# Attention with memory slots and a routed feed-forward: two sets of four batches become batches that start eight chunks apart, in an order computed by a time model

## The chip, the cores and the metric

One Trainium2 chip, one core. The metric is device time in microseconds (us) of one execution. TensorE (PE) multiplies, its weight loads are PEld, VectorE is DVE, ScalarE is ACT, GpSimd is POOL, SyncE is SP; SP and POOL also issue the DMAs, each from a queue in program order.

## The reference

B = 8 batches, H = 8 heads, S = 576 rows, head width 64, M = 32 memory slots, D = 512, F = 1024, capacity 128. All data are float32.

```python
a = exp(phi - max(phi, axis=2));  a = a / (sum(a, axis=2) + 1e-9)     # over the 576 rows
k_m = einsum('bhsm,bhsd->bhmd', a, k);  v_m = einsum('bhsm,bhsd->bhmd', a, v)
attn = softmax(q @ k_m.T / 8)                                          # over the 32 slots
x = (attn @ v_m) as (B, S, 512)
scores = x @ w_gate
for b in range(B):                                                     # the 128 rows of highest score
    xe = x[b, top]
    out[b, top] = xe + sigmoid(scores[b, top]) * (relu(xe @ w1) @ w2)  # the other rows: out = x
```

## The kernel before

Per batch there is a chain of stages. `softmax` computes `a` with 20 DVE instructions over 128x1152 (the two halves g of the heads, 576 rows each) and shorter ones, with ACT instructions between them that it waits for. `split_v` cuts each v piece (four per batch) into a high part and a rest on DVE (L285, L287) and stores each part twice in the DRAM buffer `vparts` (L290, four issues a piece on POOL's queue). `keys` turns `a` with 12 transposes (L303), splits it (L309, L311), stores each part twice in `aparts` (L314), and multiplies with k (L322) to the keys kT.

`values(st)` makes v_m for a set `st` of four batches at once. One matmul takes one row s of one batch: 32 partitions (4 head pairs, high and low part of both factors) by 128 columns, and the four batches sit in four groups of 32 partitions, so four matmuls follow each other into four row groups of the array (L371). A chunk is T = 24 rows of four batches, 96 matmuls; a set has 24 chunks. Chunks go through NB = 2 pairs of buffers: two DMAs from POOL (L345) fill `v_rows`, eight from SP (L350) fill the diagonal blocks of `a_rows`, whose other entries are zero. The first set can start when four batches are keyed, the second when eight are.

`attention(b)` needs v_m of b: `centre`, `scores`, `attend` (L505, L522 on PE, L526 to L497 on DVE), `rank` (L548, L566), `gather` (L585, and the chosen rows by an indirect DMA, L594). `ffn` multiplies 128 gathered rows with w1 and w2 (L610, L622, L629) and scatters the result (L636). In `attention`, `mean` waits until all 8 batches are keyed.

The order of instructions on every engine is the order in which these generators are advanced: two of the 16 jobs (8 softmax chains, then 8 attentions) are live at a time, and after each step of one, `split`, `sums` (the values), `weights` and `feed` (the feed-forward) get steps at fixed rates:

```python
jobs = [batch(b) for b in range(B)] + [attention_beside(b) for b in range(B)]
...
steps("sums", rows_summed, 1.5 if late else 4)
if late:
    steps("weights", weights, 1)
    steps("feed", feed, 0.6)
```

The functions in full:

Of the kernel before, what the change touches and what calls it, by code (L numbers as in the profile page):

```python
# [24 lines left out]

# [15 lines left out]
Y0_BIAS = 14 * 0.6931471805599453  # L41


@with_exitstack
def kernel(
# [14 lines left out]
    nc = tc.nc  # L60
# [13 lines left out]
    T = 24  # L74
    NB = 2
# [11 lines left out]
    accp = ctx.enter_context(tc.tile_pool(name="accp", bufs=1, space=PSUM))  # L87
    pss = ctx.enter_context(tc.tile_pool(name="pss", bufs=4, space=PSUM))
    ex = ctx.enter_context(tc.tile_pool(name="ex", bufs=2))
    work = ctx.enter_context(tc.tile_pool(name="work", bufs=2))  # L90
    one = ctx.enter_context(tc.tile_pool(name="one", bufs=1))

    def bank(shape, dtype=F32):
        return pss.tile(list(shape), dtype, tag="bank", name="bank")
# [3 lines left out]
    def load_phi(b):  # L98
        phis[b] = ex.tile([P, NG, S], F32, name="ph", bufs=3)
        for g in range(NG):  # L100
            nc.sync.dma_start(out=phis[b][:, g], in_=phiT[b, g])

    def load_k(b, g):
        ks[b, g] = ex.tile([PT, NPR, NC, Dh], F32, name="kb")
        nc.sync.dma_start(out=ks[b, g].rearrange("p h c d -> p h (c d)"), in_=k[b, g])

    def load_q(b, j):
        qs[b, j] = ex.tile([P, NPR, S // 2], F32, name="qb", tag="ph", bufs=3)
        nc.sync.dma_start(out=qs[b, j], in_=qT[b, :, :, j * (S // 2):(j + 1) * (S // 2)])
# [4 lines left out]
    make_identity(nc, ident)  # L114

    kT = [const.tile([P, NPR, M], F32, name=f"kT{i}") for i in range(B)]
    vbd = [const.tile([P, NG, NPR, Dh], F32, name=f"vbd{i}") for i in range(3)]


    v_rows = [rows.tile([P, T, NG, Dh], F32R, name=f"v_rows{i}") for i in range(NB)]  # L120
    a_rows = [rows.tile([P, NPR, T, M], F32R, name=f"a_rows{i}") for i in range(NB)]
    for t in v_rows + a_rows:
        nc.gpsimd.memset(t.bitcast(F32), 0.0)
    for t in vbd:
        nc.gpsimd.memset(t, 0.0)

    wg = const.tile([P, D], F32, name="wg")
    ident16 = const.tile([P, P], BF16, name="ident16")
# [5 lines left out]

    tgs = [const.tile([P, NT, 2], F32, name=f"tg{i}") for i in range(3)]

    def late_consts():
        nc.sync.dma_start(out=wg, in_=bass.AP(
            tensor=w_gate.tensor, offset=w_gate.offset,
            ap=[[0, P]] + [list(x) for x in w_gate.ap]))  # L140
# [17 lines left out]

    def constant(value):
        t = const.tile([P, 1], F32, name=f"c{len(biases)}")  # L160
        nc.gpsimd.memset(t, value)
        return t


    biases = {}
    for x in (EXP_P[2], EXP_P[1], EXP_Q[1], SQ_B, 1.0, 127 * 2.0 ** 23, Y0_BIAS):
        biases[x] = constant(x)
# [4 lines left out]
    tt, stt = nc.vector.tensor_tensor, nc.vector.scalar_tensor_tensor  # L172
    soft = {}

    def softmax(b):

        def t(name, dtype=F32):
            return ex.tile([P, NG * S], dtype, name=name)

        ph = phis.pop(b)  # L180
        r = ph.rearrange("p g s -> p (g s)")
        mx = ex.tile([P, NG], F32, name="mx")
        nc.vector.tensor_reduce(mx, ph, axis=AX.X, op=ALU.max)  # L183
        for g in range(NG):
            nc.vector.tensor_scalar(out=ph[:, g], in0=ph[:, g], scalar1=mx[:, g:g + 1],
                                    scalar2=EXP_LOWEST, op0=ALU.subtract, op1=ALU.max)
# [3 lines left out]
        for ln2 in (LN2_HI, LN2_LO):  # L190
            stt(out=r, in0=q, scalar=-ln2, in1=r, op0=ALU.mult, op1=ALU.add)
        act(rh, r, 1 / GRID)
        num = t("num")
        act(num, r, SQ_S, SQ_B, AF.Square)
# [601 lines left out]
```

## Time and profile before

| | before |
|---|---|
| runs of the kernel | 911.61 us median of 3 (907.06 to 912.07) |
| profiled execution, its own time | 907.15 us |
| span in its trace | 905.3 us |
| PE / DVE / ACT / POOL busy | 547.1 / 548.2 / 222.6 / 258.7 us |
| DMA | 165.55 MB, mean 183 GB/s |

The span is what the trace covers; the execution's own time has 1.85 us more. Busy shares are averages over stages with different limits; the stages are told apart in the slices and windows below.

### The profile page before, as it was taken

How to read it: one execution, taken by the hardware profiler on the slowest of the kernel's cores; microseconds unless marked ns; L12 is line 12 of the kernel's file. 1: busy time of each engine (PE TensorE's matmuls, PEld its weight loads, DVE VectorE, ACT ScalarE, POOL GpSimd, SP SyncE). 2: the span in 40 equal slices, each digit the busy share in tenths (PEclk: the TensorE clock that was granted, in tenths of full speed). 3: DMA queues.
4: the chain of work that ended last, by engine and by line, in shares of the span. 5: the costliest groups of instructions: out<-in, count | busy, mean ns of one | idle time of the engine just before them, and what ended most of it. 6: DMA issues, size and time to landing. Idle time of an engine off the chain costs nothing.

```text
span 905.3 us, 16762 instructions
## 1 busy us (share of the span) xinstructions
PE 547.1 (60%) x6917; PEld 449.3 (50%) x6918; DVE 548.2 (61%) x803; ACT 222.6 (25%) x369; POOL 258.7 (29%) x373
## 2 busy tenths in 40 slices
PE   0010020202066568774859999987999798598595
PEld 0010020202065568774728787865885675476373
DVE  8997999999965386655914336206225347748800
ACT  2423242525213124222310120300210223134210
POOL 7245353425335224224142213223223011101100
PEclk9999999999999555557585555868569799589888
DMA  3569899896998677857777755546255433111200
GB/s 103 169 246 321 267 310 293 268 306 228 292 266 259 173 226 233 225 172 210 239 214 224 233 171 167 159 125 209 69 165 175 123 94 99 64 38 64 76 21 18
DMA packets 61409, 165.55 MB, mean 183 GB/s; under 512 B 12816, under 2 KB 21008, under 8 KB 61328
## 3 DMA queue, kind: packets, MB, share of 16 engines
q0 software_dynamic: 30080, 108.02, 37.2%
q1 hardware_dynamic: 31248, 56.39, 21.3%
q8 instruction: 57, 0.93, 0.4%
q14 instruction: 24, 0.20, 0.1%
HBM read 96.21 MB, written 68.16 MB: 182 GB/s over the span
## 4 chain that ended last, share of the span: by engine, by line
PE 45%; DVE 27%; DMA 15%; SPq 5%; issue 4%; POOL 1%; ACT 1%; DVEq 0%; POOLq 0%; ACTq 0%
PE acc L371 19%; PE bank L622 8%; DMA a_rows<-aparts 7%; PE bank L629 5%; SPq L350 5%; PE bank L522 4%; DMA aparts<-aS 3%; PE bank L505 3%; DVE mx L183 2%; DMA vparts<-vlo 2%; DVE vlo L287 2%; PE bank L585 2%; DVE ph L252 2%; DMA aparts<-alo 1%; PE bank L303 1%
## 5 line engine op out<-in xcount | busy, mean ns | idle before, releaser
L371 PE MATMUL acc<-a_rows,v_rows 32*128 32x128 f32 x4608 | 234.5, 374 | 114.1 <-DMA a_rows<-aparts 87.8
L371 PEld LDWEIGHTS acc<-a_rows,v_rows 32*128 32x128 f32 x4608 | 220.0, 285 | 142.6 <-issue 125.3
L345 POOL DMA_DIRECT2D v_rows<-vparts x96 | 92.4, 967 | 287.6 <-PE acc L371 278.6
L303 PE MATMUL bank<-ident,ph 128*96 128x128 f32 x96 | 23.3, 421 | 148.5 <-DVE ph L254 148.5
L303 PEld LDWEIGHTS bank<-ident,ph 128*96 128x96 f32 x96 | 17.5, 197 | 152.2 <-issue 145.6
L622 PE MATMUL bank<-xeT,w 128*128 128x128 f32 x512 | 78.4, 309 | 2.6 <-ACT xeT L612 2.1
L622 PEld LDWEIGHTS bank<-xeT,w 128*128 128x128 f32 x512 | 70.5, 216 | 8.3 <-ACT xeT L612 3.2
L290 POOL DMA_DIRECT2D vparts<-vlo x64 | 35.6, 559 | 123.6 <-DVE vlo L287 112.6
L566 DVE SCALAR_TENSOR_TENSOR marks<-row,tg,wide 128x576 bf16<-128x576 f32 x40 | 32.7, 818 | 58.6 <-ACT row L552 57.2
L526 DVE TENSOR_TENSOR xj<-bank,rd 128x512 f32<-128x512 f32 x40 | 27.3, 688 | 62.6 <-PE bank L522 62.4
L629 PE MATMUL bank<-w,hT 128*128 128x512 f32 x128 | 65.1, 647 | 0.0
L522 PE MATMUL bank<-vbd,eT 128*128 128x256 f32 x160 | 58.6, 505 | 0.3 <-ACT vbd L430 0.3
L206 DVE TENSOR_TENSOR num<-num,lin 128x1152 f32<-128x1152 f32 x16 | 21.7, 1358 | 37.8 <-ACT lin L170 36.5
L522 PEld LDWEIGHTS bank<-vbd,eT 128*128 128x128 f32 x160 | 36.7, 248 | 11.9 <-issue 5.0
L290 POOL DMA_DIRECT2D vparts<-vb x64 | 35.9, 565 | 9.6 <-DMA aparts<-aS 9.3
L629 PEld LDWEIGHTS bank<-w,hT 128*128 128x128 f32 x128 | 25.0, 206 | 24.2 <-issue 23.0
L533 POOL DMA_DIRECT2D out<-xj x24 | 16.2, 673 | 60.7 <-DVE xj L529 44.9
L634 DVE SCALAR_TENSOR_TENSOR ye<-bank,gr,xe 128x512 f32<-128x512 f32 x8 | 6.0, 748 | 43.7 <-PE bank L629 43.7
L430 ACT ACTIVATE vbd<-bank 32x128 f32<-32x128 f32 x32 | 8.6, 268 | 96.2 <-PE bank L426 95.9
L510 DVE TENSOR_SCALAR rd<-bank 128x40 f32<-128x40 f32 x8 | 1.6, 199 | 50.5 <-PE bank L505 50.5
L564 ACT ACTIVATE marks<-row,tg 128x576 bf16<-128x576 f32 x40 | 30.9, 773 | 1.3
L322 PE MATMUL bank<-kb,aS 96*32 96x64 f32 x768 | 19.3, 285 | 17.7 <-ACT aS L304 17.7
(128 smaller groups left out, 938.3 us busy)
## 6 DMA issues: line engine op xcount, KB each, us to landing
v_rows<-vparts POOLq DMA_DIRECT2D x96, 384.0 KB, 5.8
vparts<-vlo POOLq DMA_DIRECT2D x64, 288.0 KB, 4.3
vparts<-vb POOLq DMA_DIRECT2D x64, 288.0 KB, 5.2
a_rows<-aparts SPq DMA_DIRECT2D x384, 48.0 KB
vb<-in_v SPq DMA_DIRECT2D x32, 288.0 KB
kb<-in_k SPq DMA_DIRECT2D x16, 576.0 KB
aparts<-alo POOLq DMA_DIRECT2D x32, 288.0 KB, 7.9
aparts<-aS POOLq DMA_DIRECT2D x32, 288.0 KB, 8.5
```

The lines of the kernel that those rows point to most:

```text
L290: nc.gpsimd.dma_start(out=view(vparts[g, b, t, w], c), in_=src)
L303: nc.tensor.transpose(out=tp[:, c], in_=a[:, c0 + c], identity=ident)
L345: nc.gpsimd.dma_start(out=vr[g::2, :, g], in_=vparts[g, b0:b0 + SET].rearrange("b t w j s d -> (b t w j) s d")[:, ss])
L350: nc.sync.dma_start(out=ar[2 * j + g::8, j].rearrange("p s m -> p (s m)"), in_=aparts[g, j, b0:b0 + SET].rearrange("b t w s m -> (b t w) ( ...
L371: nc.tensor.matmul(out=accs[bb][:, :P].rearrange("p (j m) -> p j m", m=M), lhsT=vr[p, s].rearrange("p g d -> p (g d)"), rhs=ar[p, :, s], s ...
L505: nc.tensor.matmul(out=den[:, c, g], lhsT=eT[:, g, c * P:(c + 1) * P], rhs=heads_of, start=True, stop=True)
L522: nc.tensor.matmul(out=o[:, g * 4 * Dh:(g + 1) * 4 * Dh], lhsT=eT[:, g, (c0 + c) * P:(c0 + c + 1) * P], rhs=vbd[b % 3][:, g].rearrange("p ...
L526: nc.vector.tensor_mul(x[:, c].rearrange("p (h d) -> p h d", d=Dh), o.rearrange("p (h d) -> p h d", d=Dh), rd[:, c0 + c].unsqueeze(2).to_b ...
L564: nc.scalar.activation(sign, row, AF.Sign, bias=g, scale=-1.0, accum_out=less[:, c:c + 1])
L566: nc.vector.scalar_tensor_tensor(out=cmp, in0=row, scalar=g, in1=wide[:, off:off + S], op0=ALU.is_equal, op1=ALU.mult, accum_out=equal[:, ...
L622: nc.tensor.matmul(out=ps[:, f, :n], lhsT=w1_sb[d][:, (f0 + f) * P:(f0 + f + 1) * P], rhs=xeT[:, d, :n], start=(d == 0), stop=(d == KD - 1))
L629: nc.tensor.matmul(out=ps[:n], lhsT=hT[:, f, :n], rhs=w2_sb[f // 2][:, f % 2], start=(f == 0), stop=(f == KF - 1))
```

## The change

1. **Lagged batches.** `values` is one walk over 88 chunks of T = 18 rows. Batch b enters at chunk 8b and leaves 32 chunks later, so chunks 0 to 7 hold one batch, 8 to 15 two, 24 to 63 four, and 80 to 87 one again. The result of batch b is there at chunk 8b + 31. The roles of the two operands are swapped (a is the stationary one), so v_m takes one more transpose per batch.
2. **Compact rows, widened on chip.** Four DMAs from SP bring the chunk's compact `a_flat` (NF = 3 buffers); one POOL instruction and three ACT instructions of 128x576 multiply it with a 0/1 column (`block_of`) into the four blocks of `a_rows`.
3. **v stored once.** `vparts` and `aparts` hold each part once; the loads read it twice by a stride of zero. 64 instead of 128 stores of v, 32 instead of 64 of a.
4. **Order from a time model.** Every engine call goes through `Noted`, which adds a modelled duration to that engine's modelled time (`Plan`); `in_order_of_time` always advances the generator whose next step is ready first. Two softmax chains (batches 0, 2, 4, 6, 7 and 1, 3, 5) and two attentions are live side by side. `split_v` starts a piece at the earliest every 11 modelled us.
5. **Feed-forward.** `forward` starts when all v pieces are split, all weights have come and batch 7's `a` is turned (its buffer becomes hT), and is advanced when nothing else has PE's next free time.
6. Smaller: PSUM banks are taken and given back by hand, `mean` no longer waits for all batches, the score of a pair of row tiles is made one tile at a time, in `keys` the matmuls go through one head after the other, and the cast to `ident16` and the 28 warming matmuls are gone.

```diff
+    def array(self, cycles, used, mode):
+        start = max(self.free.get("pe", 0.0), self.t if self.last in (None, "pe") else self.end)
+        per = self.speed(start)
...
+def in_order_of_time(plan, jobs):
+    live = [[0.0, bias, job, None] for bias, job in jobs]
...
+        x = min(able, key=lambda x: max(x[0], plan.free.get("pe", 0.0)) if x[1] is None else x[0] - x[1])
...
-    T = 24
-    NB = 2
+    T = 18
+    NB, NV, NF = 2, 2, 3
+    LAG = S // T // SET
+    COLS = ((B - 1) * LAG + S // T) * T
...
-        nc.vector.tensor_copy(ident16, ident)
...
             for w, src in enumerate((lo, vb)):
-                for t in range(2):
-                    nc.gpsimd.dma_start(out=view(vparts[g, b, t, w], c), in_=src)
+                nc.gpsimd.dma_start(out=view(vparts[g, b % SET, :, w, c0:c0 + S], c), in_=src)
...
+    def a_loader():
...
+                    nc.sync.dma_start(
+                        out=a_flat[ch % NF][32 * r0 + 2 * t + g:32 * r1:4]
+                            .rearrange("p s m -> p (s m)"),
+                        in_=src[:, ch * T * M:(ch + 1) * T * M].unsqueeze(1)
+                            .to_broadcast([(r1 - r0) * NPR, 2, T * M]))
...
+    def v_loader():
...
+            while ch - NV >= len(used_up) or len(flat) < ch:
+                yield lambda: ch - NV < len(used_up) and len(flat) >= ch
...
+                nc.gpsimd.dma_start(
+                    out=v_rows[ch % NV].bitcast(F32)[32 * r0 + g:32 * r1:2, g]
...
+    def widener():
...
+                if j < 1:
+                    nc.gpsimd.tensor_scalar_mul(ar[:, :, j], src, block_of[:, j:j + 1])
+                else:
+                    nc.scalar.activation(ar[:, :, j], src, AF.Copy, scale=block_of[:, j:j + 1])
...
+    def values():
+        for ch in range(COLS // T):
...
+            for s in range(T):
+                for b in live(ch):
+                    p = slice(b % SET * 32, b % SET * 32 + 32)
+                    nc.tensor.matmul(out=accs[b % SET][:, :P].rearrange("p (g d) -> p g d", d=Dh),
+                                     lhsT=ar[p, s].rearrange("p j m -> p (j m)"), rhs=vr[p, :, s],
...
-        while len(keyed) < B:
-            yield
...
+    def forward(count, general=False):
+        if not general:
+            while sum(x for x, _ in split) < B * NG * VC or len(w2_sb) < KF or B - 1 not in turned_away:
...
+    in_order_of_time(plan, [
+        (1 * 1e3, chain([0, 2, 4, 6, 7], 0)), (1 * 1e3, chain([1, 3, 5], 1)),
+        (1.5 * 1e3, keys()), (0.0 * 1e3, split_v()),
...
+        (0.0 * 1e3, values()), (0.0 * 1e3, attentions(0)), (0.0 * 1e3, attentions(1)),
+        (None and None * 1e3, forward(B * nt)), (0.0, load_weights())])
```

## Rows read from the trace of the kernel before

**Rows 1.** The page: the span in 40 equal slices of 22.6 us, busy tenths.

```profile
PE   0010020202066568774859999987999798598595
DVE  8997999999965386655914336206225347748800
PEclk9999999999999555557585555868569799589888
```

**Rows 2.** Windows: length, PE, PEld, DVE, ACT, POOL busy us (instructions), PEclk, DMA share, GB/s.

```profile
100.00:150.00 50.00, 6.28 (x109) 4.86 (x109) 48.49 (x60) 17.42 (x20) 23.57 (x40) 1.00 0.87 296
452.00:905.00 453.00, 383.94 (x3841) 297.98 (x3840) 190.68 (x397) 81.43 (x208) 87.09 (x106) 0.75 0.41 126
650.00:700.00 50.00, 49.90 (x634) 39.08 (x632) 20.07 (x35) 6.42 (x17) 14.41 (x15) 0.78 0.51 154
800.00:850.00 50.00, 45.90 (x254) 33.37 (x254) 35.79 (x69) 10.64 (x27) 6.59 (x9) 0.93 0.17 61
```

**Rows 3.** Lines on DVE: busy us, mean ns of one, idle before.

```profile
L204 DVE SCALAR_TENSOR_TENSOR num<-num,ph 128x1152 f32<-128x1152 f32 x16 | 21.7, 1354 | 0.2
L252 DVE SCALAR_TENSOR_TENSOR ph<-rh,sm,ph 128x576 f32<-128x576 f16 x32 | 26.1, 816 | 0.9 <-ACT rh L247 0.4
L287 DVE TENSOR_TENSOR vlo<-vb,vlo 128x576 f32<-128x576 f32 x32 | 24.3, 758 | 1.1
L285 DVE TENSOR_SCALAR vlo<-vb 128x576 int32<-128x576 int32 x32 | 15.1, 473 | 10.5 <-DMA vb<-in_v 5.8 <-DMA vparts<-vlo 4.6
L311 DVE TENSOR_TENSOR alo<-aS,alo 96x768 f32<-96x768 f32 x16 | 15.3, 954 | 0.5
L309 DVE TENSOR_SCALAR alo<-aS 96x768 int32<-96x768 int32 x16 | 9.0, 563 | 30.0 <-ACT aS L304 30.0
```

**Rows 4.** Timeline of PE: start us, length us, line, count.

```profile
79.50 0.47 PE L328 MATMUL bank<-ident,kc 128*128 128x128 f32 x1 [10.15 <-ACT kc L326]
...
315.32 5.39 PE L371 MATMUL acc<-a_rows,v_rows 32*128 32x128 f32 x96 [1.89 <-DMA a_rows<-aparts]
...
696.44 2.90 PE L371 MATMUL acc<-a_rows,v_rows 32*128 32x128 f32 x96
...
729.64 0.72 PE L459 MATMUL bank<-qb,kT 64*32 64x288 f32 x16
...
736.39 2.29 PE L505 MATMUL bank<-heads_of,eT 128*128 128x4 f32 x20
...
740.85 1.03 PE L522 MATMUL bank<-vbd,eT 128*128 128x256 f32 x4
...
880.64 7.41 PE L622 MATMUL bank<-xeT,w 128*128 128x128 f32 x64 [0.69 <-ACT xeT L612]
...
887.89 7.03 PE L629 MATMUL bank<-w,hT 128*128 128x512 f32 x16
```

**Rows 5.** By tile: ns min/median/max, first and last start; last line: tile v_rows.

```profile
L371 PE MATMUL acc<-a_rows,v_rows x4608: 263/410/472, 251.3 to 720.8; 32*128 32x128 f32 x192
...
L303 PE MATMUL bank<-ident,ph x96: 417/417/468, 57.6 to 452.2; 128*96 128x128 f32 x96
...
L380 ACT ACTIVATE v_m<-acc x8: 272/281/298, 449.8 to 721.6; 128x128 f32<-128x128 f32 x8
...
DMA to landing us min/median/max: 4.4/5.8/12.7
```

**Rows 6.** Timeline of the first 20 us: DVE beside POOL.

```profile
1.27 5.24 POOL L123 MEMSET v_rows<- 128x3072 f32 x2
1.35 12.09 DVE L141 CAST ident<-ident 128x128 bf16<-128x128 f32 x1 [1.35 <-POOL ident masks.py:199]
```

**Rows 7.** Lines on ACT and POOL.

```profile
L345 POOL DMA_DIRECT2D v_rows<-vparts x96 | 92.4, 967 | 287.6 <-PE acc L371 278.6 <-PE bank L426 5.2 <-DMA aparts<-alo 1.8
L247 ACT ACTIVATE rh<-ph,sm 128x576 f16<-128x576 f32 x16 | 11.5, 768 | 73.4 <-DVE sm L241 73.4
L147 POOL TENSOR_SCALAR_AFFINE_SELECT wide<-wide 128x1088 bf16<-128x1088 bf16 x1 | 1.2, 1186 | 0.1
```

More of the change, by code (lines that the diff above doesn't have):

```diff
@@ L1 @@
+import sys
 from contextlib import ExitStack
@@ L44, with alone @@
+def alone(job):
+    for got in job:
+        assert not callable(got) or got()
 @with_exitstack
@@ L96, with first_free, take, lock @@
+    def first_free():
+        slot = min(banks, key=lambda x: x[0])
+        banks.remove(slot)
+        plan.t = max(plan.t, slot[0])
+        return Bank(slot)
+    def take(n=1):
+        while len(banks) < n:
+            yield lambda: len(banks) >= n
+        got = [first_free() for _ in range(n)]
+        return got if n > 1 else got[0]
+    def lock(name):
+        while name in held:
+            yield lambda: name not in held
+        held.add(name)
     phis, ks, qs = {}, {}, {}
     def load_phi(b):
-        phis[b] = ex.tile([P, NG, S], F32, name="ph", bufs=3)
+        phis[b] = ex.tile([P, NG, S], F32, name="ph", tag=f"ph{b % 3}"), plan.t
@@ L100, in load_phi @@
         for g in range(NG):
[L101 to L109, printed above, removed]
+            nc.sync.dma_start(out=phis[b][0][:, g], in_=phiT[b, g])
@@ L111 @@
+        phis[b] = phis[b][0], plan.end
     load_phi(0)
     ident = const.tile([P, P], F32, name="ident")
-    make_identity(nc, ident)
+    make_identity(tc.nc, ident)
     kT = [const.tile([P, NPR, M], F32, name=f"kT{i}") for i in range(B)]
[L117 to L123, printed above, removed]
@@ L271, in ask @@
             nc.sync.dma_start(out=vb, in_=view(v[b, g], c))
-            asked.append(vb)
-        done = []
+            asked.append((vb, plan.end))
+        done, stored = [], [0.0, 0.0]
+        yield 8e3
         ask()
@@ new lines, in keys, with live, slots @@
+            bk = yield from take()
+            nc.tensor.transpose(out=bk([P, P]), in_=kc, identity=ident)
+            yield
+            copy(kT[b].rearrange("p j m -> p (j m)"), bk([P, P]))
+            bk.give()
+            keyed[b] = max(plan.end, written)
+    keyed = {}
+    n_pieces = S // T
+    def live(ch):
+        return [b for b in range(B) if b * LAG <= ch < b * LAG + n_pieces]
+    def slots(ch):
+        if len(live(ch)) == SET:
+            return 0, SET
+        return live(ch)[0] % SET, live(ch)[-1] % SET + 1
@@ L453, in scores @@
         for half in range(2):
-            qb = qs.pop((b, half))
-            scs = [bank([P, N]) for g in range(NG)]
+            while (b, half) not in qs:
+                yield lambda: (b, half) in qs
+            qb, at = qs[b, half]
+            yield at
+            bks = yield from take(2)
+            scs = [x([P, N]) for x in bks]
             for j in range(NPR):
@@ L689, in batch @@
-    def batch(b):
-        if b + 1 < B:
-            load_phi(b + 1)
-        yield from softmax(b)
-    def attention_beside(b):
-        if b == 0:
-            for j in range(2):
-                load_q(b, j)
-        while b not in v_m or b and (b, 1) not in qs:
-            yield
-        if b == 0:
-            yield from first_of(b)
-        else:
-            yield from attention(b)
-    def first_of(b):
-        job = attention(b)
-        for _ in job:
-            if len(keyed) == B and not eTs:
-                for i in range(2):
-                    eTs.append(ex.tile([P, NG, NT * P], F32, name=f"eT{i}", tag="kb"))
-                    nc.gpsimd.memset(eTs[i][:, :, S:], 0.0)
-            yield
@@ L759 @@
         for b in range(B):
-            finish(attention(b, True))
-            while chosen:
-                next(feed)
+            alone(attention(b, True))
+            alone(forward(nt, True))
 def kernel(q, k, v, phi, moe_w_gate, moe_w1, moe_w2, moe_capacity):
```

1027 lines of the change are left out of this document (683 added, 344 removed).

## The prediction

> **What bounds the kernel now.** I read the slices first, then windows, then the lines and timelines of the stages. The slices show two halves [rows 1]. Up to slice 20 (452 us) DVE leads: it makes eight softmax chains, at 48.5 of 50 us while nothing else wants it [rows 2], and mostly at 5 or 6 tenths in slices 11 to 18, where the first set's values run. From 452 us on PE is busy 384 of 453 us [rows 2], but its granted clock is 0.75 of full speed, so it does 384 x 0.75 = 288 us of work at the 2.4 GHz level. I call that warm-us: 288 in 453 is a density of 0.64. The two halves are the story: DVE idles where the first set's values run, because no attention can start before a whole set is summed (first v_m copied at 449.8 us, last at 721.6 [rows 5]); and PE has hardly anything to do in the first 250 us and too much afterwards. What ends the kernel is the second half's PE work at its poor clock, then two feed-forwards alone.
>
> **What a batch costs.** DVE, softmax: 20 instructions over 128x1152 at 1.354 us are 27.1; eight over 128x576 at 0.816 are 6.5; the reduction, two subtractions and five tiny ones I put at 3.4 by the same widths: 37 us. Splitting v: 4 x (0.473 + 0.758) = 4.9; splitting a: 2 x (0.563 + 0.954) = 3.0 [rows 3]. That is 45, eight times 360. DVE's total is 548.2; less the 12.1 of the cast [rows 6] 176 stay for eight attentions: 22 each. The change adds 16 tile-wise score triples, a few us in all, and drops the cast.
>
> PE at full clock: a feed-forward takes 7.4 + 7.0 = 14.4 us, an attention's large pieces 2.29 + 5 x 1.03 + 2 x 0.72 = 8.9 [rows 4]. The whole attention follows by subtraction: 288 less 8 x 14.4 less 2304 value matmuls at 2.90/96 = 30 ns (69) leaves 104, so 13 a batch, the turned rows of the feed-forward and the warming matmuls, which go, included. The values cost 30 ns a matmul at the high level and 5.39/96 = 56 at the low one [rows 4], four row groups in rotation.
>
> **The change, part by part.**
>
> *The start.* The first reduction waits behind the cast, which took 12.1 us while POOL filled buffers [rows 6]. The cast goes; POOL's fills stay in another form and can still hold the first subtraction. The reduction ends with the cast at 13.4 us, as if it had begun at 12.1; I count 3 us gained, bounds 0 and 7, so a start at 9.
>
> *v and a stored once.* 64 + 32 stores go from POOL's queue and 27 MB from the wires. They lie beside the DVE-bound stage, so I take 0; their cover is DVE, and without it the wires at 0.87 busy [rows 2] would gain. I keep that as help for the loads below.
>
> *Widening.* Per chunk one POOL and three ACT instructions of 128x576. ACT's nearest row is 0.768 us [rows 7]: 264 x 0.768 = 203 us on ACT, 223 busy before, so 426 in some 750; not a bound. POOL: between 5.24/2/3072 = 0.85 ns an element [rows 6] and 1186/1088 = 1.09 [rows 7], 0.49 to 0.63 us, 88 times 43 to 55. POOL's queue still issues the chunk's v loads at 0.967 us each [rows 7], now 176 instead of 96, so 170 us of issues. Neither sets the end as long as a chunk takes more than 2 x 0.967 + 0.6 = 2.5 us on POOL and 2.3 on ACT; were ACT's part not hidden, the last 32 chunks would pay 74.
>
> *Keys.* Matmuls of one head follow each other, so they stay in one column group. Before, the keys tail (first turn to kT) took 57.6 to 80 us, 22 us [rows 4, 5]. PE idles there; dearer matmuls only lengthen this tail. I keep 22 and add nothing; 10 more would move the last batch by 10.
>
> *The end of the softmax stage.* Two chains and two attentions interleave, so attentions of batches 0 to 2 fill DVE now. DVE must have done 8 x 37 + 32 x 1.23 + 7 x 3 + 2.5 x 22 = 411 us when batch 7's softmax ends; at the 0.97 of the present stage [rows 2] and 9 us of start that is 433 us (378 if the attentions waited; 465 if DVE reaches 0.9). Before, the last turn was at 452.2 [rows 5], with no attention done.
>
> *The walk.* Batch 7 keyed at 433 + 22 = 455; then chunks 56 to 87 remain. A v load waits on POOL until PE is done with its buffer, as now (278.6 us of POOL's idle time [rows 7]). Behind it in that queue stand the next widening, stores of v and of the output, gathers and scatters; who waits for them is DVE's next split and the feed-forward. SP's chunk loads wait for the widening, with the loads of k, q and weights behind them. A buffer's round is 0.97 issue + 5.8 landing [rows 5] + 4.0 of its chunk's matmuls (72 at 56 ns), for two buffers: 10.8/2 = 5.4 us a chunk; at full clock 4.5. The lower bound by the fastest landing (4.4) and full clock is 3.8, the upper the first set's own pace: (449.8 - 251.3)/24 = 8.3 for 24 rows [rows 5], 6.2 scaled to 18. I take 5.4: 32 chunks are 173, last v_m at 628.
>
> *PE after 433.* Eight feed-forwards (they may not start before batch 7 is turned) 115, five and a half attentions 71, and the values of some 35 chunks. If only matmuls count, those are 1656 x 30 ns = 50. If one batch alone holds the array as long as four in rotation (no row shows one alone), they are 35 x 18 x 4 x 30 ns = 76. Sum 236 to 262 warm-us, against 288 that PE had left at 452.
>
> The Trainium skill speaks to that ("TensorE: Matmul & The Clock Gate", Part 3, The mechanism): a weight load overlaps matmuls in flight only in another row group. By it the lone batches of the last chunks pay the full 76, and the sum would be 262; the trace has four groups in rotation only, so no row here shows it.
>
> *Density.* While chunks run I take 0.78, that of the window 650 to 700 (PE busy 49.9 of 50 at clock 0.78), since feed-forwards now fill what the loads leave. Afterwards 45.9 x 0.93/50 = 0.85 [rows 2]. From 433 to 628: 195 x 0.78 = 152. Left 84 to 110 at 0.85: 99 to 129 us, so PE ends at 727 to 757. From the last matmul to the end of the span it was 905.3 - 894.9 = 10 us [rows 4]: span 737 to 767, middle 752. The execution's own time lies 1.85 above the span. Before is 907.15 by that execution, the runs' median 911.61 is 0.5% higher; a change under 0.5% could not be told from none. Forecast 754, own range 705 to 790.
>
> **Rivals.**
>
> *The path, not PE, sets the end.* If FFN and attentions pack better than 0.78, the end is last v_m 628, then an attention nearly alone (22 on DVE, 13 on PE, some 10 on ACT in sequence: 45), gather 5, feed-forward 15, end 10, outside the span 2: 705; with 4.5 us a chunk 676. For it: the time model fills PE's gaps with feed-forward. Against: PE still has 236 or more warm-us. 676 to 705.
>
> *PE no denser than before.* At 0.64 the 236 to 262 take 369 to 409: 802 to 842, plus 12: 814 to 854. For it: values matmuls went at the low clock, 5 tenths in ten of the slices 13 to 24 [rows 1]; a wrong order shows as PE waiting with work behind it.
>
> *DVE held by POOL's widening.* In the first 13 us one DVE instruction took 12.1 us beside POOL fills [rows 6]. If each of the 60 widenings up to batch 7 stops DVE for its 0.49 to 0.63 us, the softmax stage ends 29 to 38 us later: 783 to 792. The rule stands in the Trainium skill ("SBUF — State Buffer", SBUF: two separate sides): DVE with two SBUF inputs and a GpSimd instruction that reads SBUF take one pair of ports as an exclusive lock. The cast row agrees as to fills; no row has a POOL reader beside such a DVE instruction.
>
> *The walk is paced by latency (the other side).* 88 chunks replace 48. If a chunk costs a fixed time whatever its rows, the walk from 115 us (batch 0 keyed) to the last v_m takes 88 p, and 77 follow: with the first set's unscaled 8.3 us that is 115 + 730 + 77 = 922, and with the second's, at most (721.6 - 449.8)/24 = 11.3, far more. It decides from p = (907 - 192)/88 = 8.1 on. For it: landing 5.8 to 12.7 us, two buffers, POOL's one queue shared with stores. Against: in the second set PE was shared, and a chunk now needs four SP issues instead of eight.
>
> **How the numbers follow.** Forecast 0.55; path 0.16; PE no denser 0.13; DVE held 0.06; walk paced by latency 0.10, of which 0.01 falls within 0.5% of before. So faster 0.90, same 0.01, slower 0.09. The range 665 to 850 leaves out the walk (0.10) and the fringes of the others (some 0.06).
>
> **What would show it.** Right: last a turned near 433 us; v_m copies spread from about 280 to 628 instead of two bunches; some 5.4 us a chunk; DVE at 9 tenths until 430; PE at 0.75 to 0.85 warm share after it. Wrong: chunks at 8 us, with v loads landing late or POOL waiting for PE ahead of stores that others need; PE idle after 430 while feed-forwards are ready; DVE instructions longer beside POOL's; or a feed-forward start long after 433.

## The result, and the profile after

The changed kernel takes 843.08 us (median of 4 runs, 833.61 to 846.56) against 911.84 (4 runs, 907.06 to 915.98): a ratio of 0.9153, 95% interval 0.9091 to 0.9215. Forecast was 754, range 665 to 850. The direction was right; the gain is 69 us instead of 158. The profiled execution took 846.43 us, with a span of 844.6; it and one other of the four runs (846.56) fell in a slower state of the chip, which the ratio leaves out, so rows of it are compared with runs of the experiments to some 1%.

The slices of the changed kernel, to be laid beside [rows 1]:

```profile
PE   0003276989877795779889998999999999997991
DVE  5999999889998998992735547174344542624800
PEclk9999999999999999999957999997575697588996
```

PE now starts early and is never idle for long; DVE is full up to slice 18 (380 us). One warning on reading the third line: its 9s ahead of 400 us can't be taken as the high level. 72 value matmuls take 4.11 us at 278.84 and 2.23 us at 480.41 (timeline, below), and the run with the keys rotated shows the granted clock there at 0.50 (below). So PE's value matmuls ahead of 400 us run at the lower of its two levels, 1.2 GHz.

Windows of the changed kernel (columns as in [rows 2]):

```profile
100.00:200.00 100.00, 76.50 (x542) 71.53 (x542) 93.78 (x105) 65.69 (x87) 70.42 (x67) 1.00 0.55 172
200.00:300.00 100.00, 79.70 (x937) 73.47 (x935) 94.51 (x106) 63.27 (x86) 69.00 (x66) 1.00 0.81 245
412.00:820.00 408.00, 388.48 (x4167) 313.13 (x4168) 191.72 (x417) 182.82 (x356) 181.71 (x203) 0.80 0.42 131
820.00:844.60 24.60, 6.80 (x18) 2.75 (x16) 0.96 (x3) 0.44 (x1) 0.98 (x1) 0.73 0.05 14
433.00:844.60 411.60, 380.56 (x3917) 302.08 (x3917) 179.75 (x392) 169.71 (x331) 169.90 (x189) 0.80 0.39 122
```

The third row is the main one. From 412 us, when batch 7's keys are there, PE is busy 388 of 408 us at 0.80: 311 warm-us, and 5 more to the end. The forecast had 236 to 262 left at 433; by the last row 304 were left there.

ACT's timeline: when the first, second and last batch's sum leaves its accumulator (answers to the v_m copies of [rows 5]); and by tile, PE's turns of a, the last at 383.8, against a forecast of 433:

```profile
356.00 0.26 ACT L710 ACTIVATE turned<-acc 128x128 f32<-128x128 f32 x1
...
433.06 0.26 ACT L710 ACTIVATE turned<-acc 128x128 f32<-128x128 f32 x1
...
756.76 0.28 ACT L710 ACTIVATE turned<-acc 128x128 f32<-128x128 f32 x1 [8.04 <-PE acc L699]
```

```profile
L550 PE MATMUL bank<-ident,ph x96: 417/421/472, 70.5 to 383.8; 128*96 128x128 f32 x96
```

So chunks 0 to 31 took from 110 (first value matmul) to 356 us, 7.7 a chunk, and chunks 32 to 87 took 401 us, 7.2 a chunk; the forecast had 5.4 throughout, a first v_m near 280 and the last at 628. From the last v_m to the end are 88 us (forecast 124, as PE was to work on until 727 to 757).

Lines of the changed kernel that cost most on the walk (busy us, mean ns of one, idle before and its releasers):

```profile
L699 PE MATMUL acc<-v_rows,a_rows 32*128 32x128 f32 x4608 | 298.3, 346 | 34.8 <-DMA v_rows<-vparts 25.6 <-POOL a_rows L679 5.2 <-issue 3.7
L679 POOL TENSOR_SCALAR a_rows<-a_flat,block_of 128x576 fp32r<-128x576 f32 x88 | 190.0, 2159 | 2.5
L655 POOL DMA_DIRECT2D v_rows<-vparts x176 | 98.4, 564 | 197.2 <-PE acc L699 195.7 <-PE bank L934 1.3 <-issue 0.2
L590 PE MATMUL bank<-kb,aS 96*32 96x64 f32 x768 | 68.3, 308 | 27.4 <-DMA kb<-in_k 25.4 <-ACT aS L537 1.9
```

The same 4608 value matmuls occupy PE for 298 us; the line before had 234.5. The keys hold it for 68 (the line before: 19.3). The widening on POOL is 2.16 us each, not 0.49 to 0.63.

PE's timeline, four batches live (x72) and one (x18), at the high level; and below, from the chain of waits, one batch at the low level:

```profile
278.84 4.11 PE L699 MATMUL acc<-v_rows,a_rows 32*128 32x128 f32 x72
...
480.41 2.23 PE L699 MATMUL acc<-v_rows,a_rows 32*128 32x128 f32 x72
...
743.83 2.22 PE L699 MATMUL acc<-v_rows,a_rows 32*128 32x128 f32 x18
```

```profile
149.81 4.04 PE acc L699 x18
```

A chunk of a lone batch, 18 matmuls, holds the array as long as one of four batches with 72.

The last step of the keys of batches 1, 3 and 7 on PE (L597), and among them the start of chunk 8, which is the first matmul behind the 144 of chunks 0 to 7:

```profile
160.27 0.47 PE L597 MATMUL bank<-ident,kc 128*128 128x128 f32 x1 [0.31 <-ACT kc L594]
...
169.78 5.59 PE L699 MATMUL acc<-v_rows,a_rows 32*128 32x128 f32 x50 [2.27 <-POOL a_rows L679]
...
247.41 0.47 PE L597 MATMUL bank<-ident,kc 128*128 128x128 f32 x1
...
411.68 0.27 PE L597 MATMUL bank<-ident,kc 128*128 128x128 f32 x1
```

Chunk 8 starts 9.5 us behind the keys of batch 1. Chunk 24 (the row of 278.84 above) starts 31 us behind those of batch 3, and when batch 7's keys are there the walk is at chunk 36 and not at 56. So the walk follows the keys closely at first and then falls behind them; from then on it is not missing keys that hold it.

Lines of PE from the first value matmul to the first v_m (110 to 357 us), then one from 357 to 412 us, then from 412 us to the end:

```profile
L699 PE MATMUL acc<-v_rows,a_rows 32*128 32x128 f32 x1440 | 133.1, 415 | 25.7 <-DMA v_rows<-vparts 16.8 <-POOL a_rows L679 5.2 <-issue 3.7
L590 PE MATMUL bank<-kb,aS 96*32 96x64 f32 x528 | 48.5, 314 | 17.6 <-DMA kb<-in_k 17.6
L550 PE MATMUL bank<-ident,ph 128*96 128x128 f32 x66 | 17.9, 430 | 2.4 <-DVE ph L456 2.4
L597 PE MATMUL bank<-ident,kc 128*128 128x128 f32 x5 | 2.4, 475 | 5.2 <-ACT kc L594 5.2
...
L699 PE MATMUL acc<-v_rows,a_rows 32*128 32x128 f32 x328 | 19.2, 392 | 0.0
...
L699 PE MATMUL acc<-v_rows,a_rows 32*128 32x128 f32 x2844 | 146.3, 306 | 9.1 <-DMA v_rows<-vparts 8.9 <-ACT a_rows L681 0.2
...
L864 PE MATMUL bank<-vbd,eT 128*128 128x256 f32 x100 | 37.2, 517 | 0.0
...
L864 PE MATMUL acc<-vbd,eT 128*128 128x256 f32 x40 | 14.6, 506 | 0.0
```

The early walk mixes values with keys and turns on PE; 2844 of the 4608 value matmuls are still to come at 412 us, and 140 of the 160 matmuls of L864.

Lines on DVE, to be laid beside [rows 3], and the widening by tile (ns min/median/max):

```profile
L520 DVE TENSOR_TENSOR vlo<-vb,vlo 128x576 f32<-128x576 f32 x32 | 27.8, 869 | 1.1
L453 DVE SCALAR_TENSOR_TENSOR ph<-rh,sm,ph 128x576 f32<-128x576 f16 x32 | 27.7, 866 | 2.7 <-ACT rh L442 2.7
L425 DVE TENSOR_TENSOR num<-num,lin 128x1152 f32<-128x1152 f32 x8 | 12.1, 1507 | 0.1
```

```profile
L679 POOL TENSOR_SCALAR a_rows<-a_flat,block_of x88: 1715/1765/7567, 105.4 to 747.5; 128x576 fp32r<-128x576 f32 x88
```

These DVE instructions with two inputs are on average 6 to 15% longer than before (869 against 758, 866 against 816, 1507 against the 1354 of L204), and a widening lasts up to 7.6 us. The longest one, and DVE beside it:

```profile
130.85 7.57 POOL L679 TENSOR_SCALAR a_rows<-a_flat,block_of 128x576 fp32r<-128x576 f32 x1
...
131.39 1.34 DVE L386 SCALAR_TENSOR_TENSOR rl<-rh,ph 128x1152 f32<-128x1152 int16 x1
...
135.19 1.34 DVE L394 SCALAR_TENSOR_TENSOR den<-den,ph 128x1152 f32<-128x1152 f32 x1
136.46 0.45 DVE L518 TENSOR_SCALAR vlo<-vb 128x576 int32<-128x576 int32 x1
136.94 1.10 DVE L520 TENSOR_TENSOR vlo<-vb,vlo 128x576 f32<-128x576 f32 x1
```

The widening spans four DVE instructions with two inputs that keep their 1.34 us; only L520 behind them is longer, 1.10 for 0.76. So it is mostly POOL that waits, and DVE loses some tenths of a microsecond at such a meeting.

### The profile page after: what moved, and what is told of

Read it like the earlier page. It is cut to its first block, busy times and chain, and to the rows that moved or that the text cites. A ratio compares the mean times of both kernels' runs of the same rounds, so it can differ in the third digit from the quotient of the medians.

```text
span 844.6 us, 17455 instructions
## 1 busy us (share of the span) xinstructions
PE 654.8 (78%) x6898; PEld 550.0 (65%) x6898; DVE 560.2 (66%) x851; ACT 404.1 (48%) x649; POOL 395.5 (47%) x454
## 2 busy tenths in 40 slices
DMA packets 56840, 137.28 MB, mean 163 GB/s; under 512 B 11824, under 2 KB 20016, under 8 KB 56752
## 4 chain that ended last, share of the span: by engine, by line
PE 50%; DVE 20%; DMA 8%; issue 7%; POOL 7%; ACT 4%; SPq 1%; POOLq 0%; ACTq 0%; DVEq 0%
PE acc L699 20%; PE bank L1066 6%; PE bank L864 5%; PE bank L1084 4%; POOL a_rows L679 4%; DMA v_rows<-vparts 4%; PE bank L854 3%; PE acc L1084 3%; PE bank L590 2%; DMA kb<-in_k 2%; PE acc L864 2%; DVE ph L453 2%; POOL v_rows L655 2%; DVE vlo L520 1%; DVE num L398 1%
## 5 line engine op out<-in xcount | busy, mean ns | idle before, releaser
L699 PEld LDWEIGHTS acc<-v_rows,a_rows 32*128 32x128 f32 x4608 | 277.1, 256 | 81.1 <-issue 65.5
L699 PE MATMUL acc<-v_rows,a_rows 32*128 32x128 f32 x4608 | 298.3, 346 | 34.8 <-DMA v_rows<-vparts 25.6
L681 ACT ACTIVATE a_rows<-a_flat,block_of 128x576 fp32r<-128x576 f32 x264 | 184.1, 764 | 178.0 <-issue 120.3
L679 POOL TENSOR_SCALAR a_rows<-a_flat,block_of 128x576 fp32r<-128x576 f32 x88 | 190.0, 2159 | 2.5
L590 PE MATMUL bank<-kb,aS 96*32 96x64 f32 x768 | 68.3, 308 | 27.4 <-DMA kb<-in_k 25.4
L590 PEld LDWEIGHTS bank<-kb,aS 96*32 96x32 f32 x768 | 62.4, 167 | 31.2 <-DMA kb<-in_k 24.0
L524 POOL DMA_DIRECT2D vparts<-vlo x32 | 20.3, 634 | 101.2 <-DVE vlo L520 100.8
L864 PE MATMUL bank<-vbd,eT 128*128 128x256 f32 x120 | 44.8, 519 | 0.0
L1084 PE MATMUL bank<-w,hT 128*128 128x512 f32 x80 | 42.0, 663 | 0.0
L914 DVE TENSOR_TENSOR prod<-xj,wg 128x512 f32<-128x512 f32 x40 | 33.0, 825 | 0.8
L864 PEld LDWEIGHTS bank<-vbd,eT 128*128 128x128 f32 x120 | 28.8, 257 | 6.1 <-DVE xj L895 0.2
L453 DVE SCALAR_TENSOR_TENSOR ph<-rh,sm,ph 128x576 f32<-128x576 f16 x32 | 27.7, 866 | 2.7 <-ACT rh L442 2.7
```

Of the source, the lines that this page charges most:

```text
L453: stt(out=ph[:, g], in0=a0, scalar=sm[:, x, g:g + 1], in1=ph[:, g], op0=ALU.mult, op1=ALU.add)
L590: nc.tensor.matmul(out=km[jj * M:(jj + 1) * M], lhsT=aS[g][:, jj, c], rhs=kb[:, j, c], start=(c == 0), stop=(c == NC - 1))
L679: nc.gpsimd.tensor_scalar_mul(ar[:, :, j], src, block_of[:, j:j + 1])
L681: nc.scalar.activation(ar[:, :, j], src, AF.Copy, scale=block_of[:, j:j + 1])
L699: nc.tensor.matmul(out=accs[b % SET][:, :P].rearrange("p (g d) -> p g d", d=Dh), lhsT=ar[p, s].rearrange("p j m -> p (j m)"), rhs=vr[p, :, s],
L864: nc.tensor.matmul(out=o([P, D])[:, g * 4 * Dh:(g + 1) * 4 * Dh], lhsT=eT[:, g, c * P:(c + 1) * P], rhs=vbd[b % 2][:, g].rearrange("p j d ...
```

## The experiments

Theory: TensorE's work sets the end, and the forecast had too little of it left when the softmax stage ended, since the early walk was slower than 5.4 us a chunk. Rivals: POOL's widening holds DVE and the walk; the loads' latency paces the walk; the order (fixed by the kernel's time model) is wrong. Times are medians, ratios are to the kernel before in the same job. The sum of batch 0 is turned at 356.0 and that of batch 7 at 756.8 in the changed kernel; "first" and "last" below are these. Some expectations still put the first sum at 366; the row above has 356.0.

**Widening off POOL.**

```
-                if j < 1:
+                if j < 0:
                     nc.gpsimd.tensor_scalar_mul(ar[:, :, j], src, block_of[:, j:j + 1])
```

> The fourth widening instruction of each chunk goes from POOL to ACT; nothing else. Theory A (POOL's widening, 2.16 us instead of the 0.6 I put down, holds its queue and DVE and so the walk before batch 0 is summed at 366 us): DVE's 128x1152 instructions go back to 1.35 us, v_m of batch 0 comes at 310 to 335 us instead of 366, and the end at 790 to 815 us. Theory B (PE is the limit of the walk from start to end: values 298 us, keys 68 us, POOL only waits for it): POOL gets idle, v_m of batch 0 stays at 355 or later and the time within 1% of 840. Rival: ACT, 67 us busier, becomes the one that is late: 850 or more.

838.61 us, ratio 0.9184 (0.9072 to 0.9296); first 336.3, last 738.8. DVE's lines of this run:

```profile
L453 DVE SCALAR_TENSOR_TENSOR ph<-rh,sm,ph 128x576 f32<-128x576 f16 x32 | 26.0, 812 | 13.7 <-ACT rh L442 13.6
L520 DVE TENSOR_TENSOR vlo<-vb,vlo 128x576 f32<-128x576 f32 x32 | 24.3, 758 | 1.1
L425 DVE TENSOR_TENSOR num<-num,lin 128x1152 f32<-128x1152 f32 x8 | 10.8, 1350 | 0.0
```

Each is back at its length of before, the last turn of a comes at 372.0 instead of 383.8, the whole walk 18 to 20 us sooner. So POOL did hold DVE. But the end gains 4 us by the medians and nothing by the ratios (0.9184 against 0.9153): the first sum is near the range of theory A, the end is that of theory B.

**Keys' products in another order**, so that two column groups alternate:

```
-                    for j in range(2):
-                        jj = 2 * h + j
-                        for c in range(NC):
+                    for c in range(NC):
+                        for j in range(2):
+                            jj = 2 * h + j
```

> The matmuls of keys go over the two heads of a piece in turn, row slice by row slice, instead of one head after the other, so two column groups alternate. Theory A: PE's keys line falls from 68 to about 35 us, the time stays at 830 to 845. Theory B (PE limits the walk early): some 33 us of PE go before 412 us and the end comes 15 to 35 us earlier, 805 to 825.

831.65 us, 0.9028 (0.8867 to 0.9188); the products hold PE for 42.1 us instead of 68.3. First 352.0, last 746.5. The window 250 to 300 us of this run, with its records whole, shows the low level in the early walk:

```profile
250.00:300.00 50.00, 34.69 (x479) 31.00 (x480) 46.40 (x53) 30.34 (x42) 31.68 (x30) 0.50 0.81 242
```

It was run again with more rounds:

> The kernel with the keys' products in rotated order again, with more rounds, beside the same runs of the kernel before: if its 831.65 us were an accident of the run, the ratio to before comes back to 0.915 (the changed kernel's); if the 26 us that the keys' products lose on TensorE are worth something, it stays at 0.905 or below.

839.25 us, 0.9182 (0.9137 to 0.9227). The gain did not repeat: 26 us of PE's early work are worth a few microseconds at most.

**Both edits.**

> Both edits. Theory A: as the widening on ACT alone, 790 to 815. Theory B: as the rotation alone, 805 to 825. If each holds a part: below both, 770 to 795.

839.30 us, 0.9164 (0.9050 to 0.9278); first 333.0, last 739.8. Two early savings don't add up to one at the end.

**A truer price in the time model** for POOL's widening; only the order changes:

```
-                plan.note(name, 200.0 + 0.9 * cells(out), 0.0)
+                plan.note(name, 1770.0 if op == "tensor_scalar_mul" else 200.0 + 0.9 * cells(out), 0.0)
```

> Only the time model changes: POOL's widening is charged 1.77 us (its median in the trace) instead of 0.72. The instructions are the same, their order differs. Theory C (the wrong price put instructions in the wrong order, and queues wait for it): 815 to 830. Theory A and B: within 1% of 840.

855.72 us, 0.9310 (0.9114 to 0.9506); first 344.5, last 755.0. Slower, if anything.

**A lone batch priced as measured**; again only the order changes:

```
-            cycles, used = 64.0, N * K / P
+            cycles, used = 256.0 / self.together, N * K / P
...
+                plan.together = len(live(ch))
```

> Only the time model changes: a value matmul is charged 256 cycles over the number of batches live, so a lone one four times as much as now, as the trace of the change shows. If the order suffers from the missing charge: 820 to 832. Otherwise within 1% of 840.

865.25 us, 0.9518 (0.9422 to 0.9613); first 396.9, last 771.1. A true price gave a worse order: the first sum came 41 us later.

**Half the bytes of each chunk's loads** (9 of 18 rows; the others keep what the buffer held), modelled time kept:

```
-                        out=a_flat[ch % NF][32 * r0 + 2 * t + g:32 * r1:4]
+                        out=a_flat[ch % NF][32 * r0 + 2 * t + g:32 * r1:4, :T // 2]
...
-                    out=v_rows[ch % NV].bitcast(F32)[32 * r0 + g:32 * r1:2, g]
+                    out=v_rows[ch % NV].bitcast(F32)[32 * r0 + g:32 * r1:2, g, :T // 2]
```

> Each chunk loads only the first 9 of its 18 rows of v and a (the other rows of the buffers are stale); every instruction, its order and its modelled time stay. 28 of 137 MB go. Theory D (the wires, 0.78 to 0.91 busy from 200 to 400 us, pace the walk until batch 0 is summed at 366 us): v_m of batch 0 at 320 to 340 us, end at 790 to 815 us. Theory P (work and order on PE set both): v_m of batch 0 within 10 us of 366, end within 1.5% of 840.

824.42 us (817.03 to 833.46; before 912.65 there; no ratio, as the four runs lie 16 us apart). First 342.6, last 728.7. With the widening off POOL as well:

> Both edits: half of each chunk's rows not loaded (stale), and no widening on POOL. Alone the first gave 824, the second nothing measurable. If each hides the other (POOL and wires both hold the walk up to 366 us): v_m of batch 0 at 300 to 320 us and the end below 800. If they add: about 820.

835.72 us, 0.9157 (0.9038 to 0.9276); first 330.4, last 737.8. By the medians the loads cost some 2%; with the other edit beside it even that is not seen in the ratio.

**Smaller chunks, more buffers.**

```
-    T = 18
-    NB, NV, NF = 2, 2, 3
+    T = 12
+    NB, NV, NF = 3, 3, 4
```

> Chunks of 12 rows in three pairs of buffers (four for a) instead of 18 in two: the same bytes, 132 chunks, more issues and widenings. Theory W or L (the round of a buffer, issue plus landing plus matmuls, paces the walk): a round is shared by three buffers, 18 rows take some 4 us instead of 4.6 to 7; v_m of batch 0 at 335 to 350, end 800 to 825. Theory P: within 1% of 840. If issues and widenings pace it (POOL 132 x 1.4 us, ACT 396 x 0.6): 850 or more.

846.73 us, 0.9235 (0.9139 to 0.9330); first 353.4, last 746.1. Smaller chunks with a third buffer bring nothing; a third buffer for chunks of 18 rows was not tried.

**Weights loaded later**, at the end of the other softmax chain:

```
-        while 1 not in ended:
+        while 0 not in ended:
```

> The 4.2 MB of weights are loaded when the last softmax chain ends instead of at 300 us, where the wires are 0.8 to 0.9 busy. Theory D (wires pace the walk there): v_m of batch 0 some 10 us earlier (346 to 358) and the end 5 to 12 us earlier. Otherwise within 1% of 840.

844.56 us, 0.9288 (0.9199 to 0.9377); first 348.5, last 752.3. The first sum came 7.5 us sooner, the end did not move.

**Half of the second feed-forward product left out.**

```
+                if f % 2:
                     nc.tensor.matmul(out=ps[:n], lhsT=hT[:, f, :n], rhs=w2_sb[f],
```

> The second feed-forward product uses only every other one of its eight slices (half of the sum is left out): 8 x 3.5 = 28 us of PE work at the high clock go, all after 412 us. Theory P (PE is the bound from 412 us on): 28/0.8 = 35 us earlier, 800 to 810 us. Theory W (the walk's loads, then the last attention and feed-forward set the end, PE is busy because it is given filling): 825 to 838, only the last feed-forwards' own 3.5 us each.

835.35 us, 0.9102 (0.8973 to 0.9232); last 753.3. That is some 8 us for half of the 128 matmuls, which last 68 us in the changed kernel; theory P expected 35, and the time is in the range of theory W. The late stage, to be laid beside the third row of windows above:

```profile
412.00:820.00 408.00, 367.94 (x4008) 306.80 (x4008) 186.13 (x412) 179.05 (x350) 176.65 (x199) 0.77 0.42 130
```

The 28 warm-us are gone (283 against 311), but PE was idle for 40 of the 408 us instead of 20, and its clock was 0.77 instead of 0.80. The density fell with the work, so the amount of PE's work does not set the end by itself.

**Half of the lone batches' rows left out, late** (chunks from 64 on):

```
+                    if ch >= 64 and s % 2 and s < T - 1:
+                        continue
```

> In the chunks from 64 on (three, two and one batch live) every other row is left out of the sum: 24 x 9 x 0.12 us = 26 us of PE at the high clock, if a lone batch holds the array as long as four. Theory P: 26/0.8 = 30 us earlier, 805 to 815. If a lone matmul costs only its own 30 ns: 13 us of PE work, 818 to 828.

816.36 us (806.57 to 828.00, no ratio); last 711.6. The model's order moved with it, so it was done again with the model still charged:

```
+                    if ch >= 64 and s % 2 and s < T - 1:
+                        plan.matmul(None, ar[p, s].rearrange("p j m -> p (j m)"), vr[p, :, s])
+                        continue
```

> The same for chunks 64 to 87 (one to three live batches, parts of the sums of batches 5 to 7 missing), the order kept. 24 chunks by 8 rows by 0.120 us (2.15 us for 18 rows of a lone batch at the high clock) are 23 us at full speed, 29 at the granted 0.80. Theory A (TensorE's work alone sets the end after 412 us): the run takes 811 to 820 us. Theory B (latency of the chunks' loads paces the late walk): the last v_m turned at 750 or later, not 756.8, and 835 us or more.

815.57 us, 0.8909 (0.8849 to 0.8970): 27.5 us below the changed kernel (22 by the two ratios), where the rows' own time is 23 at full clock and 29 at 0.80. ACT's timeline, the last sum:

```profile
728.04 0.28 ACT L713 ACTIVATE turned<-acc 128x128 f32<-128x128 f32 x1 [4.60 <-PE acc L702]
```

All the loads and widenings were there, and yet the last sum came 29 us sooner. In the late walk PE's time for the values, then, is paid in full at the end.

**The same rows left out early** (chunks 0 to 23), first with the model's order free, then with it kept (`ch >= 64` becomes `ch < 24`):

> In chunks 0 to 23, where one to three batches are live, every other row is left out of the values (8 of a chunk's 18), so part of the sums over positions is missing for batches 0 to 2; the loads, the widening and all else stay. 24 chunks by 8 rows by 0.224 us (a row of a lone batch, 4.04 us for 18) are 43 us of TensorE. Theory A (the early walk is bound by TensorE): the first v_m is turned 25 to 43 us earlier, at 314 to 332 instead of 357, and the run takes 805 to 825 us. Theory B (the loads, the widening and the keys hold the early walk, and TensorE has room): the first v_m is turned at 345 or later, and the run takes 832 us or more.

832.46 us (813.54 to 834.54, too far apart for a ratio; before 922.17 there); first 325.2, last 738.9.

> As the run with half of the lone batches' early rows left out (chunks 0 to 23, 8 of a chunk's 18 rows, part of the sums of batches 0 to 2 missing), but the kernel's time model is still charged for them, so that each engine's order stays that of the changed kernel. 43 us of TensorE's work at the low clock go before the first v_m, which was turned at 356.0 there. Theory A (TensorE's own work sets the pace of the early walk): turned at 313 to 330, and every later v_m 25 to 43 us earlier; 800 to 818 us. Theory B (loads, widening and the order's waits set it): turned at 340 or later; 830 us or more. Between the two: shared.

831.49 us, 0.9083 (0.9020 to 0.9145). ACT's timeline, first and last sum, then the window 200 to 300 us (for its clock of 1.00 the warning above holds) and SP's longest wait between 180 and 345 us:

```profile
347.18 0.26 ACT L713 ACTIVATE turned<-acc 128x128 f32<-128x128 f32 x1
...
740.96 0.28 ACT L713 ACTIVATE turned<-acc 128x128 f32<-128x128 f32 x1 [8.04 <-PE acc L702]
```

```profile
200.00:300.00 100.00, 66.91 (x770) 58.89 (x768) 99.11 (x110) 65.00 (x89) 68.23 (x68) 1.00 0.83 251
```

```profile
SPq L631 <- ACT a_rows L681: 50.2, 14, 7.9
```

43 us of PE's work gone brought the first sum only 8.8 us forward; PE's idle time in that window rose from 20 to 33 us. DVE stood at 99, and SP's loads of a waited 50 us on ACT's widening (26 in the changed kernel). ACT widens in the order of its queue, between pieces of the softmax that themselves wait for DVE; that fits these waits, but no run took it away. With the order kept, then, TensorE does not pace the early walk; with it free, 31 of 43 us came back at the first sum.

**More matmuls early**: a product of 128x128 by 128x128 after every third row of chunks 0 to 39, its result never read, the model not charged:

```
+                if s % 3 == 2 and ch < 40 and banks:
+                    slot = min(banks, key=lambda x: x[0])
+                    if slot[0] <= plan.t:
+                        tc.nc.tensor.matmul(out=slot[1][:, :P], lhsT=ident, rhs=ident,
+                                            start=True, stop=True)
```

> Up to chunk 39, after every third row of a chunk, one more fp32 product of 128x128 by 128x128 goes to TensorE if a bank is free; its result is never read, and the kernel's time model is not charged for it. In the two runs whose records are whole there (the one with the keys rotated, and the one with the truer price for the widening), the granted clock is 0.50 between 300 and 350 us, and the first v_m is turned at 350 to 366. Theory A (before the first v_m the walk is bound by TensorE at its low clock, and more filling raises the clock as the feed-forward does later): the clock between 200 and 350 us rises to 0.7 or more, v_m[0] is turned before 345, the run takes 800 to 830 us. Theory B (the clock there is not set by how full TensorE is, or the walk waits for other things than TensorE): the products only add their own time to a full engine, or fill its gaps; clock 0.50 to 0.54, v_m[0] at 360 to 420, and 840 to 890 us.

954.01 us, 1.0366 (1.0289 to 1.0443); first 462.0. The window 200 to 300 us:

```profile
200.00:300.00 100.00, 100.00 (x616) 80.12 (x614) 55.68 (x63) 44.65 (x60) 41.08 (x46) 0.50 0.44 136
```

PE is busy all the time and the clock stays at 0.50: the filling gave back nothing, and first sum and end came later than either theory had them. The filling's line from 110 to 463 us:

```profile
L706 PE MATMUL bank<-ident 128*128 128x128 f32 x380 | 145.8, 486 | 0.0
```

These 145.8 us lie ahead of the first sum; they delay it by 106. So PE has some 40 us of slack there, and the idle time in the changed kernel's lines from 110 to 357 us says much the same: 25.7 + 17.6 + 2.4 + 5.2, some 51.

> The extra products of the run with extra products early, together with the keys' products in rotated order (831.65 us alone, 42 us of TensorE for the keys instead of 68). Theory A (low clock holds the early walk): 790 to 820 us, faster than either alone. Theory B: within 10 us of the run with the extra products alone, and slower than the rotated order alone by 5 us or more.

949.84 us, 1.0264 (1.0160 to 1.0368); first 455.4. As the second theory has it.

**Feed-forward held back** until all sums are done:

```
-            while sum(x for x, _ in split) < B * NG * VC or len(w2_sb) < KF or B - 1 not in turned_away:
+            while sum(x for x, _ in split) < B * NG * VC or len(w2_sb) < KF or B - 1 not in turned_away \
+                    or len(summed) < B:
```

> The feed-forwards start only when the last v_m is summed; the walk shares PE with the attentions alone. If the walk's pace of 7.1 us a chunk after 412 us comes from sharing PE with feed-forwards (some five of eight run there): last v_m at 680 to 700 us instead of 758, and then eight feed-forwards of 15 us and the end, 815 to 835 us: nearly the same time by another way. If the pace is that of the loads: last v_m stays at 745 to 758 and the end is 870 to 885.

920.76 us, 1.0148 (1.0062 to 1.0234); last 763.1. The window in which the late walk runs without feed-forwards, and the values in it:

```profile
412.00:762.00 350.00, 316.63 (x3412) 271.58 (x3411) 160.68 (x350) 160.00 (x304) 162.10 (x186) 0.56 0.45 140
```

```profile
L699 PE MATMUL acc<-v_rows,a_rows 32*128 32x128 f32 x2844 | 198.7, 383 | 21.1 <-DMA v_rows<-vparts 12.3 <-POOL a_rows L679 8.4
```

Without feed-forwards between the chunks the walk is not a microsecond faster: PE is still busy 90% of the time, now at 0.56 instead of 0.80, and the same 2844 value matmuls hold it for 198.7 us instead of 146.3. Both expectations failed on the end, which came 36 us behind the later of them. In this kernel the feed-forwards inside the walk are largely paid for by the clock that PE had with them among the chunks.

## Why the prediction was wrong, point by point

*What bounds it, density, the end.* Right in the main. PE is busy 388 of the 408 us from 412 on, and what the values were spared late came back in full. But half of the second feed-forward product gave 8 us of 35, so the end is not the work left over a fixed density. The density came out at 0.76 (311 in 408) for a forecast of 0.78 and later 0.85. The range of the rival "PE no denser than before", 814 to 854, holds the measured time by chance: its density was 0.64 and its work 236 to 262. The end set by the path, at 676 to 705, did not happen.

*The start, the stores.* The first subtraction begins at 9.17 us on DVE, 13.50 before: 4.3 us gained for 3. The bytes fell from 165.55 to 137.28 MB, 28 for 27.

*The end of the softmax stage.* Forecast 433, measured 383.8, near the lower bound ("378 if the attentions waited"; its own terms give 376): no attention could run ahead of the first sum at 356, and the forecast had two and a half in it. Batch 7's keys were there at 412 instead of 455.

*The walk.* This is the step that failed, in the sentence "Batch 7 keyed at 433 + 22 = 455; then chunks 56 to 87 remain", with its price of 5.4 us a chunk. It let the walk keep up with the keys; at 5.4 from 110 us on, 56 chunks would have been done at 412. Chunks 36 to 87 hold 2880 value matmuls, and 2844 lay behind 412 us: 20 chunks more than forecast. The price of 5.4 us a chunk was the round of two buffers, as if PE were free for the walk. Up to the first sum PE alone needed 133 us for values and 69 for keys, turns and kT, 202 of 247, or 6.3 a chunk; on top came the waits of widening and loads behind a full DVE. No one of these waits accounts for the rest: the widening off POOL moved the first sum by 20 us, half the bytes by 13, half the lone rows by 9 with the order kept. From 357 to 412 us, beside the last keys and the first attention, it did only 328 matmuls, four and a half chunks. After 412 us it shared PE with everything else, at 6.6 a chunk (52 in 345 us), and "one chunk per round" had no meaning there.

*PE after 433.* Mis-sized as a consequence: 316 warm-us left at 412 and 304 at 433, not 236 to 262. What follows is arithmetic with mean densities, not an experiment. Values: 52 chunks at 2.23 are 116, forecast 50 to 76. Attentions: 140 of 160 matmuls of L864 are seven batches at 13, 91, forecast 71. Against the middle of the forecast, 249, 67 warm-us were missing; at the measured density of 0.76 they are 88 us. The density itself costs some 18 (249 warm-us at 0.76 instead of 0.78 and 0.85), the last stretch some 8 (PE's last matmul ends at 826.8, 17.8 us ahead of the end of the span instead of 10). That is, to rounding, the 113.6 us by which the stage grew (432.6 from 412 to the end of the span, against 319 from 433); 21 of it is offset by the earlier start, and 752 + 92.6 is the span measured.

*A lone batch.* The upper bound, "one batch alone holds the array as long as four in rotation", held: 2.22 us for 18 and 2.23 for 72. The Trainium skill ("TensorE: Matmul & The Clock Gate", Part 3, The mechanism) says that a weight load overlaps matmuls only in another row group; this case's trace agrees. The middle of 50 and 76 was the wrong choice here, for 24 chunks early and 24 late have fewer than four batches.

*Keys.* "PE idles there; dearer matmuls only lengthen this tail" was wrong in its ground: with the walk under way PE doesn't idle there. They cost PE 49 us more than before. That this cost little at the end (the rotated order gave 0 to 11 us) is shown; that it belongs to PE's slack ahead of the first sum is what the two runs with early rows left out and with extra matmuls say.

*Widening.* The price on ACT held (0.764 us for 0.768); that on POOL was 3.4 to 4.4 times too low. DVE was held, as one rival had it, but by 12 us at the end of the softmax stage instead of 29 to 38, and by 4 at most at the end. The Trainium skill ("SBUF — State Buffer", SBUF: two separate sides) calls the shared port pair an exclusive lock, held for the whole instruction. The widening of 7.57 us that waited beside four DVE instructions agrees with that; the DVE instruction at its end lost 0.34 us, though, and not the 1.7 us that the shortest widening lasts. The row of the cast, which the forecast called in agreement, has one input beside fills that read nothing, so it is no case of the rule that the forecast gave.

*The walk paced by latency.* It came close to its deciding pace (7.7 and 7.2 against 8.1) but not by its mechanism: a third buffer with smaller chunks, and half the bytes, changed the end by some 2% at most, and rows left out late, with every load in place, gave their full time back.

What stays open: which wait sets the early walk with the order as it is, and why the density fell when feed-forward work was left out. No version tried beats the changed kernel beyond doubt.

## What to carry to other kernels

Before a stage is priced by its buffers' round, add up what each engine must do in that stage at the clock that it will have there, the neighbours' work included; the larger of the two is the pace. Then ask how much work is left when the other bound falls away: what the early stage does not do is paid later, here at some 1.3 us for each warm-us by the mean density. The late rows bear that out (27.5 us for 23 warm-us), half of the second feed-forward product does not (8 us for 28). And a saving in an early stage with several limits close together is worth little by itself: edits that spared PE 26 to 43 us, or brought the first sum 9 to 31 us forward, moved the end by 4 to 19 by the medians, and by 11 at most where there is a ratio.

## What the runs showed of the hardware

- TensorE's granted clock was 0.50 over 100 us in which it was busy 100.00 with values, keys and 128x128 products of an identity. In the late walk it was 0.80 with feed-forwards among the chunks and 0.56 without them, and 2844 value matmuls took 146.3 and 198.7 us. Holding the feed-forwards back cost 78 us by the medians.
- 18 matmuls of 32 rows in one row group took as long (2.22 us) as 72 in four (2.23).
- A POOL multiplication of 128x576 from f32 to fp32r took 1.715 us at best, 7.567 at worst beside DVE; beside it one line of DVE's 128x1152 with two inputs (L425) took 1.507 us on average, 1.350 with the widening elsewhere.
- The issue of a v load of up to 288 KB on POOL took 0.564 us, one of 384 KB 0.967 before [rows 7]; landing took 3.6 us in the median (5.8 before [rows 5]).
- The order matters by itself: two orders made from truer prices were 1.5 and 2.6% slower by the medians than the one from wrong prices; the second lies clear of the changed kernel's interval (0.9422 to 0.9613 against 0.9091 to 0.9215), the first does not.
